# Value windows loaded as 64 and 32 rows, with the rows between zeroed on chip for the first batch, and a new order table

## The chip, the cores and the metric

The kernel runs on one core of one Trainium2 chip. The metric is device time in microseconds (us) of one execution; lower is better. Before the change three runs gave 452.86 us as the median (451.57 to 452.99).

TensorE (PE in the profile) multiplies matrices, VectorE (DVE), ScalarE (ACT) and GpSimd (POOL) work element by element, and SyncE (SP) issues all transfers. Each engine runs its own instructions in the order in which the program lists them, and waits for other engines and for transfers at semaphores.

## The reference

Attention over 8 heads feeds a gated two-layer network. Everything is float32 except the three weight matrices, which arrive as 64-bit numbers.

```python
# attention: q, k, v are (4, 8, 768, 64); block = 32, window = 16
k_sum = k.reshape(B, H, nb, block, D).max(axis=3)
v_sum = v.reshape(B, H, nb, block, D).mean(axis=3)
scores_l = scale * np.matmul(q, k.transpose(0, 1, 3, 2))
mask_l = np.abs(pos[:, None] - pos[None, :]) < window
scores_s = scale * np.einsum('bhsd,bhnd->bhsn', q, k_sum) + np.log(block)
scores_all = np.concatenate([np.where(mask_l, scores_l, -1e9), scores_s], axis=-1)
a = softmax(scores_all)                      # over 768 + 24 columns
x = a @ np.concatenate([v, v_sum], axis=2)   # heads side by side: (4, 768, 512)
# network: d_model 512, d_ff 1024
x_prev = x shifted by one token, zeros first
xk, xr = mu_k * x + (1 - mu_k) * x_prev, mu_r * x + (1 - mu_r) * x_prev
out = sigmoid(xr @ w_r) * (np.maximum(xk @ w_k, 0) ** 2 @ w_v)
```

Each query sees its neighbours within 15 positions and, besides, 24 block keys (the maximum of 32 keys each), whose values are the 24 block means.

## The kernel before

**Attention.** Two heads share the 128 partitions, so a batch has 4 pairs. The 768 tokens are 12 windows of 64 queries. A window uses 120 keys: 64 of its own stretch, the 24 block keys, and the 32 that follow. The array of values lies in memory in the same pattern, 128 rows a window: rows 0 to 63, then 24 rows of zeros (64 to 87), then 32 rows (88 to 119), and 8 rows more of zeros. `load_set` (L391) brings, for one pair of heads, the keys (`kt`, L398) and the values of two half sequences (`vx`, L403, one transfer of all 128 rows and 384 KB each). VectorE takes maxima of the keys (L423 to L431) and writes the 24 block keys into the gaps (L435, on VectorE or GpSimd). The 24 rows of block means go into rows 64 to 87 of the values: in the first batch TensorE sums the windows (L447), ScalarE and TensorE move the sums (L454 to L457) and GpSimd or VectorE spreads them over the windows (L461); in the later batches VectorE sums a second, transposed copy of the values (L379, L381), TensorE turns it (L384), and a transfer from `vm` to `vx` spreads the means (L468).

`unit` (L473) is the attention of one pair of heads and one half sequence, 32 of them in all: 24 small score products (L487), mask and maximum on VectorE (L497), exponential on ScalarE (L501), a division by the sum (L512, L518 or L523), three transposes on TensorE a head (L535), copies out (L541, L543), 24 small products with the values (L550), and a copy out (L564, L565).

**Network.** Three products stand for each product of full precision: weights and activations are split into a high and a low part. The weights are made from 64-bit words on chip in 20 pieces (L318 to L361) during the first batch, by VectorE, ScalarE and GpSimd. For each batch and half sequence `gate` (L629, products at L637 to L639) and `experts` (L654, products at L666 and L691, the last ones at L717) do the dense work.

**Order.** A planner records about 1930 operations. The table `ORDER` (L65) lists them in the order in which they are to be issued, with a letter where an operation goes to an engine other than its usual one (D, A, P). `schedule` (L200) walks through the table with assumed lengths (`LENGTH`, L39), mode changes (`SWITCH`, L54) and latencies, and assigns buffers; the engines keep that order. Its start times serve one more purpose: where the plan sees TensorE idle ahead of the first large products, L763 puts products of a zeroed tile with itself (`av<-still`, L764, called products on zeros here), one per 230 ns of planned idle time. They compute nothing that is used.

The lines that set this, in short:

```python
            if b or not SPLIT:
                op("SP", "load", lambda hf=hf: nc.sync.dma_start(
                    out=vw[hf].t[:, 0:S].rearrange("p (w d) -> p w d", d=P), in_=v[b, p, hf]), ...)
                continue
            op("POOL", "vzero", zeros(nc.gpsimd), writes=[(vw[hf], "b")], other=("DVE", "vzero_d", zeros(nc.vector)))
            for x, lo, hi in (("a", 0, QW), ("c", KB, NK)):
                op("SP", "load", lambda hf=hf, lo=lo, hi=hi: nc.sync.dma_start(...))
```

Of the kernel before, what the change touches and what calls it, by code (L numbers as in the profile page):

```python
# [29 lines left out]
HW = NW // 2  # L30
NSL = HW // 2
HT = S // 2
# [7 lines left out]
    score=776, transpose=245, vtrans=82, vpool=800, vsel=75, values=848, mixe=1400, gate=2780, gate_p=2085, e1=2085,  # L40
    e2a=1390, e2b=695, e2=695, e2h=350,
# [12 lines left out]
SWITCH = dict(MS=100, SM=112, MV=108, VM=112, TM=85, ST=55, VT=55, TS=175, TV=175)  # L54
LATENCY = dict(M=201, S=265, V=236, T=228, DVE=115, ACT=133, POOL=180, SP=0)
# [3 lines left out]
WARM = 230  # L59
# [7 lines left out]
209 215 217 254 79 11P 13 7D 60 279 72 14 61 8 218 219 43 221 6 15P 42 44 54D 220 45 230 55 16 53 222 304 34 241 231  # L67
223 81 80 237 239 233 33P 224 26 235 35 92 56 232 238 236 242 3 234 36 27 57P 240 28 225D 62 29 243 30 244 58 63 37 38
64 31D 245 9D 226 65 246 46 247 2 47 228 48 255 248 83 82 49 419 51 249 328 400 256 250 99 727 257 266 84 262 260 85P
264 258 267 261 265 50 280 259 263 420 251 74 283 291 401 281 287 285 73P 268 269 289 284 66 282 75 253A 305 67 270D  # L70
68 271D 76 292 290 272 403 69 609 286 312 273D 70 288 106 316 314 402 274 71 421 293 423 86 308 294 275 94 310 306 93
276 422 87 296 95 295D 424 88 329 89 299 412 302 277 90 332 300D 352 101 309 278A 404 405 334 425 701 1169 307 317 315
426 297 120 427 298 311 406 102 96 97 428 413 108 340 313 407 336 330 98 408 338 100P 318 335 337 333 77 319 320 109
113 301 103 78 353 303A 322 104 409 122D 321D 107D 668 105 431 341 339 331 148 110 414 323 123 410 342 115 354 358 411
343 356 121P 111 429 324 415 432 344 430 433 325 112 116 345 326 124 114 434 346 127 376 134 125P 435 362 364 360 150D
126 417 347 151 149 117 327A 436 162 667 152 118 136D 129D 119 418 153 437 447 440 416 135 438A 137 154 130 348 349
448 141 377 138 613 164D 439 139 350 365 441 128D 165 669 176 725 618 445 140 131 446 454 163P 380 388 382 351 143 449
442 363 355 450A 155 166 132P 641 378 384 386 443A 361 359 452 444 133 451 144 455 357 379 366 367 142D 178D 387 381
389 502 369 498 453 461 462 368D 167D 179 169 385 383 168 145 459 372 373 463 177 460 612 157 370 371 390D 468 503 158
391 180 676 601 146 464A 181 614 392D 394 456 393 374 499 615 182 619 465 395 670 156P 469 396 457A 500 475 91 643 197  # L80
626 630 624 397 671 171D 159 458 620 375A 504 160 506 147 398 501 628 476 466 611 399A 161 622 510 629 470 631 507 467
511 473 508 505 512 509 513 623 170 474 172 621 471A 514 173 183 199D 477 174 198 200 625 627 175 729 190 480 472 201
602 185 481 515 632D 186 672 184 516 605 603 187 528 188 478A 192D 673 189 193 479 520 633 487 517 191 194 529 202 518
610 599 524 195 525 634 196 521 604 644 526 519 527 636 530D 783 482 522 532 531 533 637 534 653 523 488 535 483 203
600 484 485A 562 1173 486 649 651 647 606 495 496 492 607 489 493 490 536 555 654 650 608 728 648 652 655 730 645 646
656 635 657D 658 1113 617 734 616 638 537 677 639D 660 686 538 640 678 682 688 684 679 689 539A 687 659P 663 642 680
541 664D 683 540 542 543 681 685 548 556D 544 545 690 557 661 691 549D 692P 702 662 699 693P 786 665 1053 675 1045 841
1172 842 731P 694 666 757 674 1487 546 707 703 713 785 695 704 550 759 1062 791 705 547 551 709 708 553 843D 706 1174
711 863D 710 554 712 714 696 715 735 697 552 716 1057 558 718D 717 698 792 744 1056 726 732 497 491 719 700A 742 560
787 563 743 745 559 788 740 789P 738 736 569 741 720 815 845P 737 746 739 747 846 1058 1059 864 748 721 749 750P 760  # L90
722D 494 733 751D 723 763 817 1497 784 765 570 766 752 561 761 1049 771 865 767 768 567 769 844 770 753D 764 867P 762
568 847D 772 866 773D 754 564 724 793 755 774 775D 565A 571 756 776P 798 804 794 777 800 576 802 801 790 848 1229 1046
795 758A 778 796 797 849P 779 574 566 1500 577 578 799 1501 871D 805 803 583 575 579A 868 780D 806 572 807 580 850 872
1050 781 818 584D 808 829 1111 821 573 585 810 825 823 819 1171 1112 581 811 1175 809 782A 827 1043 822 1047 582 1502
586A 1087 1236 812 828 1063 826 820 813D 814 869D 1064 824 851 1070 1072 1073 830 588 1085 1066 816A 1074 587 852 1075
589 853P 831 1067 832 834D 854 593 596 855 856 1048 1114 875P 1068 837 590 833 591 1065 876 838 1069 1071 877D 861 594
1044 878 835 873D 874 597 1088 836 598 839 1051 859 1052 1118 592 595 1095 1091 870 884 857 1115 1076 1092 942 1177
1077 943 1099 1488 1227 1097 1089 1119 860 879 1054 1120 1503 858 946D 1078D 1098 1231 880D 947 1096 1100 948 1060 881
1079D 1116 1117 1145 885D 886 882A 944D 1235 887 1090 883 950D 840A 1093 945 968D 888 969 951 891 892 862 898 919 1080
1259 920D 893 1081 952 953 972D 1121 1130 949 1094 1082 889 1132 890 1126 1128 896 1124 894A 895 1101 973 1122 1230  # L100
899 1129 1083 1133 954D 905 897 900 901 1125 1127 1170 902 955 903 1123 956D 1102 1103D 921 1131 1134D 957 906 907 904
964D 965 1146 908A 1135 1055 909 1104D 1084 1105 1556 1491 912 1157 1178 1153 1158 913 1613 1106D 1154 1061 1203 910
1136D 958 911 1107 917 959 914 960 1151 1108 915 1617 916 1155 1137 1149 1147 922A 1086A 918 1138 961 962 1150 1148
1156 924 974D 975 923 1152 963 1109 976 1179 1139 966 1616 1140 926 1618 977 978 1232 1186 1180 1182 1110A 967 1188
925 1159 1189 1160 1619 927 928 970D 929A 1141 1161D 931 1190 979 1184 1285D 1286 1287D 1185 1191 932 1204 1187 1162D
1492 1142 1555 971 1261 1489 1176 1163 930 933 936 980 1181 1164 1183 1192D 1559 1193 1194P 1143 1493 1165 1195 981
1144A 982 1213 1205 1206 939 992 1166 1311P 983A 1703 934 1558 937 938 1499 1560 1561P 985 1209 984 1210 1288 993 1215
1312 1307 940 999 986D 987 1313D 1214 1308 988A 994 989 990 1233 1000 1211 1207 1001 1289 1314 1290 991 1196 1167 1208
# [762 lines left out]
```

## Time and profile before

| | |
|---|---|
| median of three runs | 452.86 us |
| the profiled execution, its own time | 453.34 us |
| its span, first to last instruction | 451.5 us |
| TensorE busy | 443.9 us (98% of the span) |
| VectorE, ScalarE, GpSimd busy | 295.9, 284.2, 45.9 us |
| mean granted TensorE clock | 0.999 |
| products on zeros, in the trace | 122 records, 18.2 us |
| transfers | 51.95 MB; 43.28 MB read from memory |

Times in the views are microseconds from the span's first instruction unless marked ns. In a row of the timeline the first number is the start, the second how long it lasted, then come engine, line, operation, what is written `<-` what is read, shapes, and the count of instructions merged; a bracket gives idle time before it and what ended that. A float32 product of the listing is two records in the trace. Records of TensorE overlap, so the distance from start to start tells what one costs. In the views by windows each engine has its busy time and its number of instructions, then the granted clock, the share of the transfer engines in use, and GB/s.

### The profile page before, as it was taken

To read this page: it belongs to the slowest core of one execution; us is meant where nothing else is said; L and a number is where in the kernel's file an instruction comes from. 1 tells how busy PE (TensorE), PEld (TensorE's weight loads), DVE (VectorE), ACT (ScalarE), POOL (GpSimd) and SP (SyncE) were. 2 spreads that over 40 slices of the span, in tenths; PEclk is the share of its full clock that TensorE was granted. 3 is DMA by queue.
4 is the path that set the end of the run, shared out by engine and by line. 5 is a ranking of instruction groups with operands and counts; after the bars stand their busy time and mean duration, and the time that the engine had idled before them with its cause. 6 is when DMAs were issued, how large, how long until landed. Compare 5 with 4: busy or idle time off the path is not lost.

```text
span 451.5 us, 9681 instructions
## 1 busy us (share of the span) xinstructions
PE 443.9 (98%) x3608; PEld 381.6 (85%) x3608; DVE 295.9 (66%) x944; ACT 284.2 (63%) x843; POOL 45.9 (10%) x96
## 2 busy tenths in 40 slices
PE   9999999999999999999999999999999999999996
PEld 8867888789888789888988879888889888989985
DVE  2999999997887877828677676358364533445131
ACT  2889999987775849569574586466675434232211
POOL 0443222000230100000200001011002000000000
PEclk9999999999999999999999999999999999999999
DMA  8976684551557543240723112105100000003002
GB/s 311 403 262 221 208 326 131 179 208 33 145 169 217 220 132 91 85 147 1 221 73 120 53 56 84 43 19 177 48 2 0 2 0 1 0 1 116 1 0 93
DMA packets 26878, 51.95 MB, mean 115 GB/s; under 512 B 2512, under 2 KB 14416, under 8 KB 26832
## 3 DMA queue, kind: packets, MB, share of 16 engines
q1 hardware_dynamic: 26832, 51.35, 33.8%
q8 instruction: 28, 0.46, 0.4%
q14 instruction: 18, 0.15, 0.1%
HBM read 43.28 MB, written 6.29 MB: 110 GB/s over the span
## 4 chain that ended last, share of the span: by engine, by line
PE 76%; DVE 9%; ACT 8%; DMA 3%; issue 2%; SPq 1%; DVEq 0%; POOL 0%; POOLq 0%
PE mm L666 25%; PE mm L691 23%; PE av L550 4%; PE pt L535 4%; PE mm L637 4%; PE mm L639 4%; PE mm L638 4%; PE sc L487 4%; PE mm L717 3%; DMA kt<-in_k 2%; ACT y L501 2%; PE av L764 2%; DMA vx<-vm 1%; DVE y L497 1%; DVE we L336 1%
## 5 line engine op out<-in xcount | busy, mean ns | idle before, releaser
L666 PE MATMUL mm<-xs,wk_h 128*128 128x384 f32 x512 | 101.4, 340 | 0.0
L501 ACT ACTIVATE y<-y,mn 128x120 f32<-128x120 f32 x192 | 74.1, 388 | 30.5 <-DVE mn L497 30.1
L666 PEld LDWEIGHTS mm<-xs,wk_h 128*128 128x128 f32 x512 | 89.6, 188 | 3.7 <-ACT r L672 0.8
L691 PE MATMUL mm<-wv_h,kh 128*128 128x512 f32 x168 | 67.5, 402 | 0.0
L691 PE MATMUL mm<-wv_l,kh 128*128 128x512 f32 x168 | 66.3, 395 | 0.0
L497 DVE CUSTOM_DVE_ANT_0 y<-sc,fixed_sb 128x120 f32<-128x120 f32 x192 | 46.5, 276 | 25.5 <-PE pt L535 13.3
L666 PE MATMUL mm<-xs,wk_l 128*128 128x384 f32 x256 | 55.2, 337 | 0.0
L676 ACT ACTIVATE r<-r 128x384 f32<-128x384 f32 x64 | 32.9, 521 | 27.7 <-DVE r L674 27.2
L691 PE MATMUL mm<-wv_h,kl 128*128 128x512 f32 x168 | 49.1, 401 | 0.5 <-DVE kl L681 0.5
L681 DVE TENSOR_TENSOR kl<-r,kh 128x384 fp32r<-128x384 f32 x64 | 35.3, 556 | 19.1 <-ACT kh L680 11.1
L666 PEld LDWEIGHTS mm<-xs,wk_l 128*128 128x128 f32 x256 | 45.5, 188 | 0.0
L672 ACT ACTIVATE r<-mm 128x384 f32<-128x384 f32 x39 | 19.1, 489 | 38.8 <-PE mm L666 31.0
L590 DVE SCALAR_TENSOR_TENSOR xa<-vx,fixed_sb,xa 128x384 f32<-128x384 f32 x60 | 37.0, 622 | 9.1 <-ACT xa L583 7.4
L637 PE MATMUL mm<-wr_h,xs 128*128 128x512 f32 x96 | 39.0, 407 | 0.0
L639 PE MATMUL mm<-wr_h,xs 128*128 128x512 f32 x96 | 38.0, 396 | 0.0
L638 PE MATMUL mm<-wr_l,xs 128*128 128x512 f32 x96 | 37.9, 395 | 0.0
L596 DVE TENSOR_TENSOR xs<-xa,xs 128x384 fp32r<-128x384 f32 x60 | 33.0, 558 | 6.9 <-ACT xs L593 5.6
L691 PEld LDWEIGHTS mm<-wv_h,kh 128*128 128x128 f32 x168 | 31.6, 188 | 6.5 <-ACT kh L680 0.4
L691 PEld LDWEIGHTS mm<-wv_l,kh 128*128 128x128 f32 x168 | 31.6, 188 | 6.0
L501 ACT ACTIVATION_READ_ACCUMULATOR y<-y,mn 128x1 f32 x192 | 36.5, 190 | 0.0
L691 PEld LDWEIGHTS mm<-wv_h,kl 128*128 128x128 f32 x168 | 30.7, 188 | 6.8 <-DVE kl L681 0.9
L535 PE MATMUL pt<-fixed_sb,y 128*120 128x128 f32 x192 | 33.1, 281 | 0.1
(88 smaller groups left out, 699.2 us busy)
## 6 DMA issues: line engine op xcount, KB each, us to landing
vx<-in_v SPq DMA_DIRECT2D x32, 384.0 KB, 4.1
kt<-in_k SPq DMA_DIRECT2D x15, 544.0 KB, 4.9
qt<-in_q SPq DMA_DIRECT2D x32, 192.0 KB, 3.8
out<-z SPq DMA_DIRECT2D x23, 256.0 KB, 4.2
st<-in_vT SPq DMA_DIRECT2D x12, 384.0 KB, 4.5
st<-in_w_k SPq DMA_DIRECT2D x8, 512.0 KB
st<-in_w_v SPq DMA_DIRECT2D x8, 512.0 KB
st<-in_w_r SPq DMA_DIRECT2D x4, 512.0 KB, 8.0
```

Of the source, the lines that this page charges most:

```text
L497: op("DVE", "mask", lambda h=h, i=i, var=var: nc.vector.tensor_tensor_reduce(out=y[h].t[:, i, :], in0=sc[h].t[:, i, 0:NK], in1=mask_sb[:, ...
L501: op("ACT", "exp", lambda h=h, i=i: nc.scalar.activation(y[h].t[:, i, :], y[h].t[:, i, :], AF.Exp, bias=mn[h].t[:, i:i + 1], scale=-1.0, a ...
L535: nc.tensor.transpose(out=pt.t[0:NK, i * P:(i + 1) * P], in_=y[h].t[:, i, :], identity=ident_sb)
L590: op("DVE", "mixd", lambda xt=xt, xa=xa, p=p: nc.vector.scalar_tensor_tensor(out=xa.t, in0=xt.t[:, 1 + lo:1 + lo + HT], scalar=mu_sb[:, wh ...
L596: op("DVE", "sub", lambda xa=xa, xh=xh, xl=xl: nc.vector.tensor_tensor(out=xl.t, in0=xa.t, in1=xh.t.bitcast(F32), op=ALU.subtract), reads= ...
L637: nc.tensor.matmul(ps[t].t, xh.t[:, ts], wr_h[:, p, :], start=(p == 0), stop=False)
L638: nc.tensor.matmul(ps[t].t, xh.t[:, ts], wr_l[:, p, :], start=False, stop=False)
L639: nc.tensor.matmul(ps[t].t, xl.t[:, ts], wr_h[:, p, :], start=False, stop=(p == NPAIR - 1))
L666: nc.tensor.matmul(ps.t[:, 0:HT], w[:, j, p, :], x[p][s].t, start=(n == 0), stop=(n == 11))
L676: op("ACT", "square", lambda: nc.scalar.activation(r.t, r.t, AF.Square), reads=[(r, 0)], writes=[(r, 0)])
L681: op("DVE", "sub", lambda: nc.vector.tensor_tensor(out=kl.t, in0=r.t, in1=kh.t.bitcast(F32), op=ALU.subtract), reads=[(r, 0), (kh, 0)], wr ...
L691: nc.tensor.matmul(acc[t].t, a.t[:, t * P:(t + 1) * P], w[:, j, :], start=start, stop=stop)
```

## The change

The values come in two transfers a half sequence in all four batches: rows 0 to 63 (192 KB) and rows 88 to 119 (96 KB). Rows 64 to 87 and the last 8 rows are no longer read. In the first batch rows 64 to 87 are set to zero on chip, since TensorE sums whole windows there; in the later batches nothing is written there before the block means arrive, so that the transfer of means no longer follows a load of the same rows. That takes 32 transfers more and 96 KB less for each of the 32 half sequences, and 8 zeroings, 6 on GpSimd and 2 on VectorE.

The planner's numbers change: dense products a little longer, shorter latencies after scores and values and a longer one after transposes, no cost for the change from values to dense products, later landings of transfers, and more time for issuing the transfer of means. A product on zeros now counts 430 ns up to 6 us and 230 ns after that, and the first one is planned from 1.0 us. Their number falls from 61 to 49.

```diff
-SWITCH = dict(MS=100, SM=112, MV=108, VM=112, TM=85, ST=55, VT=55, TS=175, TV=175)
-LATENCY = dict(M=201, S=265, V=236, T=228, DVE=115, ACT=133, POOL=180, SP=0)
+SWITCH = dict(MS=100, SM=112, MV=108, TM=55, TS=175, TV=175)
+LATENCY = dict(M=201, S=130, V=120, T=300, DVE=115, ACT=133, POOL=180, SP=0)
...
-WARM = 230
+WARM, WARM_COLD, COLD = 230, 430, 6000
...
-SPLIT = 0
+SPLIT = 2
+LATE = 400
...
-252 227 17 18 204 0 10 39 52 21 229 32 22 23 24 25 20 19 205 59 41 40 206 212 1 210 208 216 213 207 5D 211 4D 12D 214
+71 68D 47 22 293 92 18 17 220 0 10 43 60 27 26 25 28 29P 19 245 36 24 20 21 23 221 67 45 49 48 46 1 222 223 9 224 228
...
-                now[e] = start + DMA_ISSUE
+                now[e] = start + DMA_ISSUE + o.more[0]
                 dma = max(dma, start + DMA_START) + DMA_EACH + o.size / DMA_BYTES_PER_NS
-                o.finish = dma + DMA_END
+                o.finish = dma + DMA_END + o.more[1]
...
-            if b or not SPLIT:
+            if SPLIT == 0 or SPLIT == 1 and b == 0:
...
-            op("POOL", "vzero", zeros(nc.gpsimd), writes=[(vw[hf], "b")], other=("DVE", "vzero_d", zeros(nc.vector)))
+            if b == 0:
+                op("POOL", "vzero", zeros(nc.gpsimd), writes=[(vw[hf], "b")], other=("DVE", "vzero_d", zeros(nc.vector)))
...
-    end, early = 600, True
+    end, early = 1000, True
     for o in order:
         if o.eng == "PE" and early:
-            for _ in range(int((o.start - end) // WARM)):
+            for _ in range(int(max(0, o.start - max(end, COLD)) // WARM + max(0, min(o.start, COLD) - end) // WARM_COLD)):
                 nc.tensor.matmul(spare, still, still, start=True, stop=True)
```

The table `ORDER` is new throughout, and the same code stands 3 or 4 lines further down (L487 is L491, L764 is L768). Three places show what it does.

TensorE, from its first instruction to the scores of the second pair of heads, before (`sc` is the scores, `kt` and `qt` keys and queries):

```order
L764 MATMUL av0_146<-still_160 128x128 x21
L487 MATMUL sc0_143<-kt0_61,qt0_65 64x120 x2
L487 MATMUL sc1_144<-kt0_61,qt0_65 64x120 x2
...
L764 MATMUL av0_146<-still_160 128x128 x25
L487 MATMUL sc0_143<-kt1_62,qt1_66 64x120 x2
```

and now:

```order
L768 MATMUL av0_146<-still_160 128x128 x11
L491 MATMUL sc0_143<-kt0_61,qt0_65 64x120 x2
L491 MATMUL sc1_144<-kt0_61,qt0_65 64x120 x2
...
L768 MATMUL av0_146<-still_160 128x128 x23
L491 MATMUL sc1_144<-kt1_62,qt1_66 64x120 x2
```

Ahead of the first scores 21 products on zeros became 11, and ahead of the second 25 became 23; from there to the scores of the third pair there are 15 in both.

GpSimd, from its first tile to the first weights, before (`wc`, `we` and `wr_h` belong to the weights):

```order
L758 MEMSET still_160 128x128
L558 MEMSET vx0_68 128x1
L558 MEMSET vx1_69 128x1
L328 ISA
L328 TENSOR_SCALAR wc0_141<-st0_136 128x512
L358 TENSOR_SCALAR wr_h_157<-wc0_141 128x512
```

and now:

```order
L762 MEMSET still_160 128x128
L412 MEMSET vx0_68 24x768
L412 MEMSET vx2_70 24x768
L412 MEMSET vx3_71 24x768
L562 MEMSET vx4_72 128x1
L412 MEMSET vx5_73 24x768
L439 COPY kt0_61<-ks0_80 128x12x24
L412 MEMSET vx6_74 24x768
L335 ISA
L335 TENSOR_SCALAR we0_139<-st0_136 128x512
L361 TENSOR_SCALAR wr_h_157<-wc0_141 128x512
```

Five zeroings come ahead of the first weights on GpSimd (one more stands at the start of VectorE's row, ahead of the first maxima of keys), and the block keys of the first pair, which VectorE wrote before (L435), are written here behind four of them. The scaling of the first weights (`wc0`) went from GpSimd to ScalarE.

SyncE, the values of the first pairs, before:

```order
L318 DMA st2_138<-in_w_r 128x1024
L403 DMA vx2_70<-in_v 128x768
L403 DMA vx3_71<-in_v 128x768
L398 DMA kt2_63<-in_k 128x1088
L403 DMA vx4_72<-in_v 128x768
L403 DMA vx5_73<-in_v 128x768
L476 DMA qt2_67<-in_q 128x384
L398 DMA kt3_64<-in_k 128x1088
L403 DMA vx6_74<-in_v 128x768
```

and now:

```order
L321 DMA st2_138<-in_w_r 128x1024
L417 DMA vx3_71<-in_v 32x768
L417 DMA vx6_74<-in_v 64x768
L417 DMA vx6_74<-in_v 32x768
L417 DMA vx3_71<-in_v 64x768
L401 DMA kt2_63<-in_k 128x1088
L417 DMA vx7_75<-in_v 64x768
L417 DMA vx2_70<-in_v 32x768
L417 DMA vx2_70<-in_v 64x768
L417 DMA vx7_75<-in_v 32x768
L401 DMA kt3_64<-in_k 128x1088
L480 DMA qt2_67<-in_q 128x384
```

The eight transfers ahead of these rows are the same, but for the two pieces of the first keys, which changed places. Each load of values became two, and the keys of the third and fourth pair stand behind the same number of half sequences as before.

Over the whole program the same attention and network operations remain, but some change engines: divisions by the sum on GpSimd fall from 10 to 4 and on VectorE from 29 to 25 and rise on ScalarE from 25 to 35; loads of ScalarE's function tables fall from 22 to 18. On TensorE the dense products are cut up differently: they are followed at once by scores or values 30 times instead of 17, and values are followed at once by dense products 18 times instead of 4.

More of the change, by code (lines that the diff above doesn't have):

```diff
@@ L39 @@
 LENGTH = dict(
-    score=776, transpose=245, vtrans=82, vpool=800, vsel=75, values=848, mixe=1400, gate=2780, gate_p=2085, e1=2085,
-    e2a=1390, e2b=695, e2=695, e2h=350,
+    score=776, transpose=245, vtrans=30, vpool=800, vsel=320, values=848, mixe=1400, gate=2797, gate_p=2095, e1=2095,
+    e2a=1398, e2b=700, e2=700, e2h=350,
     kred=862, kred2=460, kmax=75, kcopy=225, vred=865, mask=203, eps_d=72, rc=100, norm3=448, evac=470, pts_d=468,
@@ L70 @@
[L70 to L89, printed above, removed]
@@ L105 @@
[L105 to L108, printed above, removed]
-1237 995A 1197 1168A 1216 1212 1198 1217 1246 1238 1506 1622 941 1494 1239 997 935 1242 1243 998 1244 1199 1248 1249
@@ L141 @@
+1917 1936 1884D 1918 1921 1922 1919 1923 1924 1925 1927 1926 1928D 1885 1929 1932 1933 1948 1930A 1937A 1938 1939 1931
+1949 1940 1941 1942 1946 1943 1950 1944 1945 1886 1947 1953 1887 1951A 1952 1955 1954 1956 1960 1957 1958 1959 1961
+1962 1965 1888 1889 1963 1966 1890 1967 1964 1515 1968 1891 1971 1969 1972 1970 1973
 """
@@ L151, with __init__ @@
 class Op:
-    def __init__(self, n, ways, bufs, size):
-        self.n, self.ways, self.bufs, self.size = n, ways, bufs, size
+    def __init__(self, n, ways, bufs, size, more):
+        self.n, self.ways, self.bufs, self.size, self.more = n, ways, bufs, size, more
         self.deps, self.start, self.finish, self.eng = set(), None, None, None
@@ L170, in buf, with op @@
         return Buf(pool, n)
-    def op(self, eng, kind, emit, reads=(), writes=(), size=0, other=()):
+    def op(self, eng, kind, emit, reads=(), writes=(), size=0, other=(), more=(0, 0)):
         bufs = []
@@ L181, in op @@
             ways = {e: w for e, w in ways.items() if w[0] not in BAN}
-        o = Op(len(self.ops), ways, bufs, size)
+        o = Op(len(self.ops), ways, bufs, size, more)
         o.tag, o.name = self.tag, kind
@@ L379, in block_means @@
             op("SP", "load", lambda p=p, tokens=tokens: nc.sync.dma_start(out=tokens(), in_=vT[b - 1, p]),
-               writes=[(vt, 0)], size=P * S * 4)
+               writes=[(vt, 0)], size=P * S * 4, more=(0, LATE))
             op("DVE", "vred", lambda p=p, tokens=tokens: nc.vector.tensor_reduce(
@@ L414, in load_set @@
                     out=vw[hf].t[lo:hi, 0:S].rearrange("p (w d) -> p w d", d=P), in_=v[b, p, hf, lo:hi]),
-                   writes=[(vw[hf], x)], size=(hi - lo) * HW * 512)
+                   writes=[(vw[hf], x)], size=(hi - lo) * HW * 512, more=(0, LATE if b else 0))
         def blocks():
@@ L469, in load_set @@
                     out=windows(x)[QW:KB], in_=means.t[NS * p:NS * p + NS].unsqueeze(1).broadcast_to([NS, HW, P])),
-                   reads=[(means, 0)], writes=[(x, "b")], size=NS * HW * 512)
+                   reads=[(means, 0)], writes=[(x, "b")], size=4 * NS * HW * 512, more=(480, 0))
         return e
@@ L476, in unit @@
         op("SP", "load", lambda: nc.sync.dma_start(out=qt.t, in_=q[b, p, :, hf * HT:(hf + 1) * HT]),
-           writes=[(qt, 0)], size=P * HT * 4)
+           writes=[(qt, 0)], size=P * HT * 4, more=(0, LATE if b else 0))
         sc, y, mn, pts = [[buf(x) for _ in range(2)] for x in ("sc", "y", "mn", "pts")]
```

126 lines of the change are left out of this document (75 added, 51 removed).

## Prediction

> **What bounds the kernel now.** I read the busy time by windows first, then the timeline of the start, then the waits of TensorE.
>
> The windows of the whole span (TensorE, its weight loads, VectorE, ScalarE, GpSimd):
>
> ```profile
> 0.00:25.00 25.00, 23.47 (x255) 21.35 (x255) 16.92 (x60) 13.85 (x50) 5.39 (x13) 1.00 0.95 360
> 25.00:65.00 40.00, 39.90 (x455) 31.45 (x454) 38.10 (x135) 39.17 (x124) 14.42 (x21) 1.00 0.72 245
> 65.00:200.00 135.00, 132.92 (x1124) 113.17 (x1125) 109.13 (x352) 102.12 (x314) 13.30 (x31) 1.00 0.46 152
> 200.00:448.00 248.00, 247.64 (x1779) 215.60 (x1777) 131.29 (x398) 129.06 (x356) 12.76 (x31) 1.00 0.15 49
> ```
>
> From 25 us on TensorE is idle for 0.1 + 2.1 + 0.4 us in all, so the time is TensorE's work plus its start and its end. Between 25 and 65 us ScalarE (39.17 of 40 us) and VectorE (38.10) are full as well: what comes later there makes TensorE wait. Behind 200 us both are about half idle. The start is different, since its busy time is mostly products on zeros. By lines they are
>
> ```profile
> L764 PE MATMUL av<-still 128*128 128x128 f32 x122 | 18.2, 313 | 1.5 <-POOL still L758 1.0 <-DVE vx L564 0.5
> ```
>
> The timeline of the start:
>
> ```profile
> 0.99 7.85 PE L764 MATMUL av<-still 128*128 128x128 f32 x42 [0.99 <-POOL still L758]
> ...
> 5.17 0.31 DVE L435 COPY kt<-ks 128x288 f32<-128x288 f32 x1
> ...
> 8.78 0.85 PE L487 MATMUL sc<-kt,qt 64*64 64x120 f32 x24
> ...
> 9.55 5.85 PE L764 MATMUL av<-still 128*128 128x128 f32 x50
> 9.68 0.28 DVE L497 CUSTOM_DVE_ANT_0 y<-sc,fixed_sb 128x120 f32<-128x120 f32 x1 [4.20 <-PE sc L487]
> ...
> 10.21 0.40 ACT L501 ACTIVATE y<-y,mn 128x120 f32<-128x120 f32 x1 [8.19 <-DVE mn L497]
> ...
> 15.33 0.85 PE L487 MATMUL sc<-kt,qt 64*64 64x120 f32 x24
> ...
> 23.55 0.30 DVE L435 COPY kt<-ks 128x288 f32<-128x288 f32 x1
> ...
> 24.38 0.49 PE L764 MATMUL av<-still 128*128 128x128 f32 x2 [0.54 <-DVE vx L564]
> ...
> 25.13 0.85 PE L487 MATMUL sc<-kt,qt 64*64 64x120 f32 x24
> ```
>
> The first keys are complete at 5.48 us, and their scores start at 8.78, when the first 21 products on zeros are through. VectorE had stood for 4.20 us, ScalarE for 8.19. The queries of that score are the other thing that it needs:
>
> ```profile
> L476 SPq DMA_DIRECT2D qt<-in_q x1: 432/432/432, 1.6 to 1.6; - x1
> ...
> DMA to landing us min/median/max: 4.5/4.5/4.5
> ```
>
> They land at 1.64 + 4.5, say 6.2 us. So the products on zeros hold up the first scores by 2.6 us, and everything in the chain behind them.
>
> **The change part by part.** *Ten products fewer ahead of the first scores.* The windows of L764 alone give their pace, 218 ns a record up to 7.1 us (28 in 6.11) and 106 ns after it (16 in 1.70), though the granted clock reads 1.00 in both:
>
> ```profile
> 0.00:7.10 7.10, 6.11 (x28) 6.11 (x29) 1.00 0.75 252
> 7.10:8.80 1.70, 1.70 (x16) 1.55 (x14) 1.00 1.03 417
> ```
>
> Eleven products are 22 records, 4.8 us, and end at 5.8. The scores then start at 6.2 to 6.3, when the queries have landed; the block keys, which GpSimd now writes behind four zeroings, are near that too (below). But the scores run in the slow phase until 7.1: 0.85 us there do what 0.41 would, so the first mask comes 0.9 + 0.4 us behind the start, at 7.6 instead of 9.68. I count -2.1 us. Without the slow phase it would be -2.5; with a start at 6.8 it would be -1.8.
>
> The Trainium skill (TensorE: Matmul & The Clock Gate, Part 1) says that the array runs at half rate until about 3.4 us of sustained activity and again after an idle window of that length, and that the window runs freely. By that figure, as an estimate, the scores at 6.2 us would be at full rate and the term -2.5 us. The trace's 7.1 us, 6.1 after the first product, is longer than the figure, and I go by the trace.
>
> *The zeroings.* The nearest row is the spread over the same 24x768 elements:
>
> ```profile
> 20.62 0.82 POOL L461 COPY vx<-vm 24x768 f32<-24x768 f32 x1 [0.68 <-ACT vm L457]
> ```
>
> Four of them from 0.9 us end at 4.2 us, ahead of the maxima of keys at 5.2, and the copy behind them is hidden by the wait for the queries: cost nothing. If one took 1.2 us, they would end at 5.7 and the scores would start 0.3 us later. The zeroing on VectorE lies in a time when it waits for keys. The other ones on GpSimd fall into its 19.6 idle us of the first 25; the second on VectorE is counted with its row.
>
> *From the first mask to the third pair's scores at 25.13.* VectorE is the chain here. By the order it does the same work up to its 24th mask: one zeroing and one copy out of `pt` more, one sign, one copy of block keys and one copy of `av` less. So the shift of 2.1 us stays. TensorE has 23 products (46 records at 117 ns, 5.4 us) behind the first scores and then 15, as before, so they don't block it. At the end TensorE loses more than VectorE: the third keys are ready at 23.85, but the scores wait 1.28 us, since a product on zeros ahead of them waits for VectorE to copy `av`. ScalarE does that copy now, sooner in its row. I take half, -0.6 (0 to -1.2).
>
> *ScalarE up to the first gate.* The scaling of a piece of weights, by lines from 9 to 65 us:
>
> ```profile
> L325 ACT ACTIVATE wc<-st 128x512 f32<-128x512 f32 x5 | 3.4, 689 | 0.0
> ```
>
> By the order ScalarE does three of these more, 2.1 us; the other shifts cancel. It starts 2.1 us earlier and has slack until 25 us (13.85 busy), not behind it. I take +0.3 (0 to +2.1).
>
> *Transfers.* A window of the start, whose last two columns are the transfer engines' share and GB/s:
>
> ```profile
> 10.00:15.00 5.00, 5.00 (x47) 5.00 (x46) 4.96 (x23) 4.28 (x19) 1.38 (x2) 1.00 1.02 408
> ```
>
> Then the issues (size, us to landing), and SyncE's wait at the transfer of means (total, times, longest):
>
> ```profile
> vx<-in_v SPq DMA_DIRECT2D x32, 384.0 KB, 4.1
> qt<-in_q SPq DMA_DIRECT2D x32, 192.0 KB, 3.8
> ```
>
> ```profile
> SPq L468 <- DMA vx<-in_v: 27.5, 9, 4.8
> ```
>
> The transfer engines are full in the start at 408 GB/s. Eight half sequences of 96 KB less are 768 KB, 1.9 us less to move, so data doesn't fall behind a chain that is 2 us earlier. Later the means no longer wait for a load: 27.5 us of SyncE's waits go. What was queued behind them (queries, keys) goes out earlier; 32 issues come in, at some 0.43 us each as that of the queries above. Nothing of that is on TensorE's path but the wait of 0.4 us below.
>
> The Trainium skill (DMA: Bandwidth & Descriptors, Anatomy of one DMA) speaks against small pieces: about 2 us fixed for each, of which 96 KB would need only 0.2 more. By that, as an estimate, a lone 96 KB reaches a tenth of the rate. Here eight are in flight and 408 GB/s is reached with pieces of 192 KB among them; the trace's own 3.8 us for 192 KB against 4.1 for 384 also says that a landing hardly depends on size.
>
> *Mode changes on TensorE.* Three stretches give the prices, from start to start:
>
> ```profile
> 48.32 0.49 PE L535 MATMUL pt<-fixed_sb,y 128*120 128x128 f32 x3
> 48.57 0.48 PE L637 MATMUL mm<-wr_h,xs 128*128 128x512 f32 x1
> 48.88 0.40 PE L638 MATMUL mm<-wr_l,xs 128*128 128x512 f32 x1
> ...
> 58.33 0.49 PE L535 MATMUL pt<-fixed_sb,y 128*120 128x128 f32 x3
> 58.74 0.85 PE L487 MATMUL sc<-kt,qt 64*64 64x120 f32 x24
> ...
> 60.37 0.50 PE L691 MATMUL mm<-wv_h,kh 128*128 128x512 f32 x1
> 60.71 0.39 PE L691 MATMUL mm<-wv_l,kh 128*128 128x512 f32 x1
> 60.94 0.40 PE L691 MATMUL mm<-wv_h,kh 128*128 128x512 f32 x1
> ...
> 95.75 0.40 PE L639 MATMUL mm<-wr_h,xs 128*128 128x512 f32 x1
> 96.08 0.85 PE L487 MATMUL sc<-kt,qt 64*64 64x120 f32 x24
> 96.85 0.54 PE L535 MATMUL pt<-fixed_sb,y 128*120 128x128 f32 x3
> 97.15 1.11 PE L666 MATMUL mm<-xs,wk_h 128*128 128x384 f32 x5
> ```
>
> A dense product takes 0.23 us among its like, 0.33 ahead of scores or values, 0.34 behind values, 0.31 behind transposes. A group of transposes takes 0.25 between dense products, 0.30 behind scores, 0.41 ahead of them. Counted through the order: dense ahead of scores or values 17 to 30 times (13 x 0.10 = +1.3), dense behind values 4 to 18 (+1.5), dense behind transposes 42 to 55 (+1.0), transposes ahead of scores or values 15 to 2 (13 x 0.16 = -2.1), transposes behind them 31 to 19 (-0.6). Together +1.1 us. It is the one certain loss.
>
> *Waits in the middle.*
>
> ```profile
> PE av L550 <- DVE pts L543: 0.6, 1, 0.6
> PE mm L691 <- DVE kl L681: 0.5, 1, 0.5
> PE av L550 <- DMA vx<-vm: 0.4, 1, 0.4
> ```
>
> The window 65 to 200 us has 2.1 us idle. The last wait ends with the freed means; the others depend on the new order, which I can't price. I take -1.0, from -2.0 to +1.
>
> The sum: -2.1 - 0.6 + 0.3 + 1.1 - 1.0 = -2.3 us. The profiled execution took 453.34 us, 1.84 more than its span and 0.5 more than the median; 453.34 would become 451.0 and the median of 452.86 becomes **450.6 us**.
>
> **The rivals.** About 0.3% (1.36 us) is what a measurement of this kernel can tell from no change.
>
> *Small pieces take the place of the products (no change).* By the program's semaphores SyncE sends a transfer when the one eight places earlier has landed. Rows 10 to 33 of its new order move 5,194 KB in 24 pieces, 216 KB on average: eight of those in 4.1 us are 432 GB/s, just above the 408 of the row. If a landing takes 5 us, the rate is 354, and these rows take 15.0 instead of 13.0 us: 2.0 us that eat the gain, 452.6 us. For it speaks that 3.8 and 4.1 us are so close; against it, that VectorE, and no landing, ended the waits in the start.
>
> *All of the products' time is saved.* The 98 records left take 4.8 + 76 x 0.117 = 13.7 us instead of 18.2. If every engine follows, the start gives -4.5 instead of -2.4: 448.5 us. For it speaks the 8.19 us that ScalarE stood, against it the full VectorE.
>
> *New waits in the three later batches (slower).* Each of 24 units there now waits for two pieces of values and the means, sent at different places of SyncE's row (of one half sequence of the second batch, 64 rows stand at row 41 and 32 rows at row 61), and scores, values and dense products alternate with less between. Without the -1.0 for the middle the gain is 1.3 us; units that wait 0.4 us like the one above use it up at the fourth, and from the seventh on the kernel is slower by more than 0.3%. If half of them wait, it is 452.86 - 1.3 + 12 x 0.4 = 456.4 us. Against it speaks the transfer engines' share, 0.46 and less after 65 us.
>
> **How the numbers follow.** Forecast 0.52, small pieces 0.18, all saved 0.17, new waits 0.13. Faster: 0.48 + 0.17 = 0.65. Same: 0.04 + 0.16 + 0.03 = 0.23. Slower: 0.02 + 0.10 = 0.12. The range goes from 448.0, all saved with a little of the middle, to 453.3, small pieces with a little more wait in the middle; it leaves out the new waits and a part of the others.
>
> **What would show it.** The first scores of the profile after start at 6.2 to 6.8 us and the first mask at 7.6; the third pair's scores at about 22.5 instead of 25.13; products on zeros 98 records, 13 to 14 us; idle time of TensorE between 65 and 200 us about 1 us; the dense products behind values at 0.34. The forecast is wrong if TensorE shows idle time of over 2 us before 25 us, or waits for `vx` in the later batches that add up to more than 3 us.

## The result and the profile after

The changed kernel takes 454.63 us (median of 20 runs, 451.93 to 458.01), the kernel before beside it 452.11 us (451.14 to 454.21). The ratio is 1.0051, with a 95% interval from 1.0031 to 1.0070: slower by 0.5%, about 2.3 us, where the forecast was 2.3 us faster. The profiled execution took 455.25 us, with a span of 453.4 us.

The windows of the changed kernel, with the columns of the prediction's (TensorE, its weight loads, VectorE, ScalarE, GpSimd, clock, share of the transfer engines, GB/s):

```profile
0.00:25.00 25.00, 21.96 (x259) 19.39 (x260) 18.29 (x63) 16.06 (x54) 9.82 (x21) 1.00 0.95 272
25.00:65.00 40.00, 35.54 (x411) 27.66 (x410) 34.78 (x118) 35.65 (x114) 11.16 (x17) 1.00 0.84 243
65.00:200.00 135.00, 134.12 (x1137) 113.94 (x1136) 113.00 (x372) 106.89 (x331) 12.13 (x23) 1.00 0.52 153
200.00:448.00 248.00, 248.00 (x1774) 215.21 (x1773) 130.75 (x404) 126.95 (x359) 8.66 (x22) 1.00 0.15 42
```

From 65 us on TensorE is idle less than before (0.9 us instead of 2.1 + 0.4). The loss lies ahead of that: 4.46 us idle from 25 to 65, where it was 0.1. Read the last two columns of the first row: the transfer engines are as full as before (0.95), but move 272 GB/s instead of 360. A share says how long packets were under way, not how much they brought.

What TensorE waits for (total, times, longest):

```profile
PE mm L451 <- DMA vx<-in_v: 4.3, 4, 1.9
PE sc L491 <- DMA qt<-in_q: 1.9, 2, 1.3
```

L451 are the block sums of the first batch, which need all rows of the values. In the timeline the first scores start at 5.82 us, before the 6.2 to 6.8 of the forecast, and the first mask at 6.72 instead of 7.6. By the third pair's scores a part of that is lost (23.55, where about 22.5 was forecast and 25.13 stood before), and the last block sums are late:

```profile
0.98 4.91 PE L768 MATMUL av<-still 128*128 128x128 f32 x22 [0.98 <-POOL still L762]
5.82 0.85 PE L491 MATMUL sc<-kt,qt 64*64 64x120 f32 x24
6.59 5.40 PE L768 MATMUL av<-still 128*128 128x128 f32 x46
...
23.55 0.85 PE L491 MATMUL sc<-kt,qt 64*64 64x120 f32 x24
...
36.62 0.96 PE L451 MATMUL mm<-vx,fixed_sb 120*32 120x128 f32 x24 [1.94 <-DMA vx<-in_v]
```

The chain of waits up to there (start, length, what) is one of transfers, each of which was only sent when the one eight places earlier had landed:

```profile
4.92 9.09 DMA st<-in_w_r
14.01 0.02 issue
14.03 7.28 DMA vx<-in_v
21.31 0.02 issue
21.33 9.01 DMA vx<-in_v
30.33 0.02 issue
30.35 6.22 DMA vx<-in_v
```

They land after 6 to 9 us, not 4 or 5. The GB/s of the stretch from 5 to 37 us, in 40 slices of 0.8 us, show since when; first the kernel before, then the changed one:

```profile
GB/s 371 422 384 412 416 405 429 402 396 424 428 388 385 406 421 411 401 389 403 401 394 396 396 388 366 288 78 108 206 262 365 405 101 65 245 385 365 338 363 77
```

```profile
GB/s 311 400 394 411 409 405 417 387 232 212 191 233 202 223 228 203 208 256 229 234 344 395 362 292 198 215 181 194 196 209 246 266 236 261 244 246 301 246 372 394
```

Some 400 GB/s until 11.4 us, and mostly about half of that from the first pieces of values on, whose first packet starts at 10.7 us. From 21.0 to 23.4 us, when only 15 of their packets start, the rate is back at 344 to 395. By 25 us 272 x 25 us = 6.8 MB have come, before 9.0; the pieces spare 0.8 MB of that, so 1.4 MB are missing, 3.4 us at 408 GB/s.

An account of TensorE up to the first dense product of the first gate, in us, from the records of each profiled execution (products on zeros, by count and us, and other work from start to start; idle: gaps over 0.15 us; the first product stands at 0.98 or 0.99). The names of the experiments stand below.

```
                        products on zeros  other work  idle  first dense product
before                    122   17.65        17.57     0.54        36.75
changed                    98   14.13        18.12     6.53        39.76
fewer products alone      102   14.79        17.57     0.79        34.13
... and pieces            102   14.41        18.19     3.84        37.43
changed, 1st batch whole  112   15.27        16.95     0.61        33.82
```

So the change saved 3.5 us of products, added 0.55 us of other work and 6.0 us of waiting, +3.0 together. Behind that product TensorE works 408.76 us before and 408.79 after, and is idle 2.13 and 0.88 us by the windows: -1.2. The sum, +1.8, is the difference of the spans (451.5 and 453.4).

### The profile page after: what moved, and what is told of

It is laid out like the page before. It is cut to its first block, busy times and chain, and to the rows that moved or that the text cites. A ratio compares the mean times of both kernels' runs of the same rounds, so it can differ in the third digit from the quotient of the medians.

```text
span 453.4 us, 9689 instructions
## 1 busy us (share of the span) xinstructions
PE 441.0 (97%) x3584; PEld 377.3 (83%) x3584; DVE 297.6 (66%) x955; ACT 286.1 (63%) x857; POOL 41.8 (9%) x83
## 4 chain that ended last, share of the span: by engine, by line
PE 88%; DMA 8%; SPq 2%; issue 0%; ACT 0%; DVE 0%; DVEq 0%
PE mm L670 29%; PE mm L695 25%; PE av L554 5%; PE mm L641 5%; DMA vx<-in_v 5%; PE mm L643 5%; PE mm L642 5%; PE pt L539 4%; PE sc L491 4%; PE mm L721 4%; DMA st<-in_w_r 2%; DMA qt<-in_q 1%; SPq L417 1%; PE mm L618 1%; SPq L480 0%
## 5 line engine op out<-in xcount | busy, mean ns | idle before, releaser
L501 DVE CUSTOM_DVE_ANT_0 y<-sc,fixed_sb 128x120 f32<-128x120 f32 x192 | 47.6, 276 | 17.7 <-PE sc L491 9.0
L676 ACT ACTIVATE r<-mm 128x384 f32<-128x384 f32 x45 | 22.1, 491 | 53.7 <-PE mm L670 48.0
L683 DVE CAST kh<-r 128x384 fp32r<-128x384 f32 x32 | 11.7, 365 | 41.9 <-ACT r L680 35.1
```

The lines of the kernel that those rows point to most:

```text
L501: op("DVE", "mask", lambda h=h, i=i, var=var: nc.vector.tensor_tensor_reduce(out=y[h].t[:, i, :], in0=sc[h].t[:, i, 0:NK], in1=mask_sb[:, ...
```

## The experiments

Times are medians, with the ratio to the kernel before, run on the same chip, and its 95% interval.

### The parts one by one

**Fewer products alone** (kernel before):

```diff
-            for _ in range(int((o.start - end) // WARM)):
+            n = int((o.start - end) // WARM)
+            for _ in range(n - 10 if n == 21 else n):
```

> The kernel before with its order and its whole value transfers, but 11 instead of 21 products on zeros ahead of the first scores. Every theory says that the first scores start at about 6.2 us. If the prediction's first term is right by itself, the third pair's scores start at 22.5 to 23.0 instead of 25.13 and the time is 450.0 to 450.5 us against 452.1. If the start is bound by the transfers, which run full at 400 GB/s there, the third pair stays at 25 and the time at 451.8 to 452.3.

449.42 us, 0.9939 (0.9918 to 0.9959). Its timeline, TensorE and VectorE:

```profile
22.52 0.85 PE L487 MATMUL sc<-kt,qt 64*64 64x120 f32 x24
...
7.10 0.28 DVE L497 CUSTOM_DVE_ANT_0 y<-sc,fixed_sb 128x120 f32<-128x120 f32 x1 [1.67 <-DMA fixed_sb<-in_fixed]
```

The third pair's scores come 2.6 us earlier, and so does the first dense product (34.13 instead of 36.75). The prediction's first term, -2.1, is there by itself, with 0.5 us to spare.

**Pieces alone** (kernel before; the rows between are zeroed once at the start, in five tiles by GpSimd and in five by VectorE):

```diff
-                op("SP", "load", lambda hf=hf: nc.sync.dma_start(
-                    out=vw[hf].t[:, 0:S].rearrange("p (w d) -> p w d", d=P), in_=v[b, p, hf]),
...
+                def pieces(hf=hf):
+                    for lo, hi in ((0, QW), (KB, NK)):
+                        nc.sync.dma_start(
+                            out=vw[hf].t[lo:hi, 0:S].rearrange("p (w d) -> p w d", d=P), in_=v[b, p, hf, lo:hi])
+                op("SP", "load", pieces,
...
+    for n, t in enumerate(pools["vx"]):
+        (nc.vector if n % 2 else nc.gpsimd).memset(t[QW:KB, 0:S], 0.0)
```

> The kernel before with its order and its 21 products, but each value transfer sent as 64 and 32 rows one behind the other, the rows between zeroed once at the start. Theory of narrow transfers (pieces on 64 or 32 partitions keep the transfer engines as busy while moving half as much): packets of 3,072 bytes take 200 to 240 ns on average before 30 us instead of 124, TensorE idles 3 us or more before 65 us, 454 to 456 us. Rival of the count (eight in flight, each transfer with a fixed cost): packets stay at 125 to 140 ns, the engines' share falls below 0.9, and the time is also 453 to 456. Rival of the order (the new order alone brings the waits): 451.5 to 452.5 us.

455.24 us, 1.0065 (1.0039 to 1.0091). The pieces alone cost 3 us, in the order before and with 25% fewer bytes of values. Packets of 3,072 bytes took 190 ns before 30 us, a little less than I had said. But the place is not the one expected: the first dense product comes at 36.39, no later than before, with 0.85 us idle ahead of it. (Its 122 products on zeros took 16.94 us instead of 17.65, since their pace changed at 5.6 us in this execution and at 7.1 in that of the kernel before.) The profile's loss stands later:

```profile
PE mm L669 <- ACT r L675: 2.1, 1, 2.1
PE pt L538 <- ACT pts L544: 1.2, 1, 1.2
```

Both lie behind 170 us, and the chain of waits leads from each back to keys of a later batch:

```profile
165.59 4.65 DMA kt<-in_k
...
213.45 6.06 DMA kt<-in_k
```

Why those keys hold up this kernel, and not the one with the same pieces in the later batches alone (below), is open.

**Fewer products and pieces**, both changes in the order before:

> The order before with 11 products and with the values in 64 and 32 rows: the changed kernel without its new order. If the effects add up: 452.1 - 2.7 + 3.2 = 452.6 us, and the new order costs the changed kernel 2 us more. If the pieces take all of the products' gain: 454.5 to 455.5, and the new order costs nothing.

451.63 us, 0.9977 (0.9957 to 0.9997), a microsecond below the first case: the pieces take 2.2 of the 2.7 us. Not all of that need be theirs. VectorE's five zeroings stand ahead of the first maxima of keys and keep it from 0.96 to 4.89 us, so that the first pair's block keys come late, and TensorE waits for them:

```profile
6.60 0.84 PE L490 MATMUL sc<-kt,qt 64*64 64x120 f32 x24 [1.14 <-DVE kt L438]
```

Without the pieces and zeroings these scores start at 5.83. How much of the 0.8 us reaches the end is not shown; with 21 products the same delay hides behind them. The same products and pieces cost 454.6 us in the new order; more on that below.

**The new order with whole transfers** (in the first batch):

```diff
...
-            for x, lo, hi in (("a", 0, QW), ("c", KB, NK)):
+            if b == 0:
+                pieces = ("a", 0, P), ("c", 0, 0)
+            else:
+                pieces = ("a", 0, QW), ("c", KB, NK)
+            for x, lo, hi in pieces:
...
```

(with nothing sent for `c`, and no zeroing, in the first batch)

> The kernel after with its order and its 11 products; the first batch's values as whole 128 rows where their 64 rows stood, without its 32 rows and its zeroings, the three later batches still in 64 and 32 rows. Theory of narrow transfers: the 6.5 us that TensorE stands between 10 and 65 us in the profile after fall to under 1.5, the middle stays at about 0.9 idle, 449 to 450.5 us. Theory that the new order is at fault too: 4 us or more of waits stay somewhere before 200 us, 452 to 454 us.

449.92 us, 0.9950 (0.9934 to 0.9967). The windows:

```profile
0.00:25.00 25.00, 23.41 (x293) 20.10 (x293) 18.46 (x72) 17.98 (x64) 8.48 (x19) 1.00 0.95 358
25.00:65.00 40.00, 40.00 (x423) 32.54 (x420) 38.46 (x129) 39.32 (x126) 9.97 (x16) 1.00 0.73 238
65.00:200.00 135.00, 132.60 (x1169) 112.50 (x1168) 108.18 (x354) 101.44 (x312) 10.66 (x22) 1.00 0.51 145
```

358 GB/s instead of 272, no idle time from 25 to 65 us, and 4.7 us won back by eight transfers that carry a third more bytes. (The zeroings are gone with them, and the planner puts 112 records of products on zeros instead of 98.) The middle did not stay at 0.9 us idle, as I had said: it is 2.4, of which TensorE waits 1.3 for queries and 1.1 for a copy by ScalarE. An earlier form used whole transfers in all four batches:

> The kernel after with its order and its 11 products, but 128 rows in one transfer where its 64 rows stood, none for its 32 rows, and no zeroing. Narrow transfers or count: TensorE's waits for values between 10 and 65 us fall from some 6 us to under 1.5, packets of 3,072 bytes take about 125 ns, 449.5 to 450.8 us. Order: the waits stay at 4 us or more and the time at 453.5 to 455.

452.35 us, 1.0016 (0.9997 to 1.0036). The waits of the start went as expected, but 4.7 us of others came between 65 and 200 us. There the new order sends the freed means of some half sequences ahead of their values, and the whole transfer writes zeros over them, so part of the later batches' means is lost. As a test of the later batches it says nothing; the next one does.

**Pieces in the later batches alone** (order before, fewer products):

```diff
...
+                    for lo, hi in ((0, QW), (KB, NK)) if b else ((0, P),):
...
```

> The order before with 11 products; values of the first batch whole, those of the three later batches in 64 and 32 rows. If narrow transfers only hurt where the transfer engines are full: 449.2 to 450.2 us, as without pieces (449.4). If the new waits of the prediction's third rival are real: idle time of TensorE behind 65 us of 3 us or more, and 451 to 453 us.

449.56 us, 0.9943 (0.9923 to 0.9962), with 0.78 us idle from 65 to 200:

```profile
65.00:200.00 135.00, 134.22 (x1134) 114.49 (x1133) 108.76 (x353) 103.11 (x311) 13.21 (x31) 1.00 0.48 142
```

Where the transfer engines are half empty the same pieces cost nothing. They also gain nothing that can be told from the 449.42 us without them.

### What makes a piece slow

Transfers of values with nothing beside them:

```diff
+STAGES = (
+    ("whole", 12, lambda i: (0, P, 0, HW)),
+    ("low64", 12, lambda i: (0, QW, 0, HW)),
+    ("rows32", 12, lambda i: (KB, NK, 0, HW)),
+    ("halves", 12, lambda i: (QW * (i % 2), QW * (i % 2) + QW, 0, HW)),
+    ("narrow", 12, lambda i: (0, P, 0, HW // 2)),
+    ("mixed", 12, lambda i: ((0, QW, 0, HW), (KB, NK, 0, HW))[i % 2]),
+    ("rows120", 12, lambda i: (0, NK, 0, HW)),
...
```

> Only transfers of values, in eight stages of twelve with a wait between stages (the output is left without a meaning): whole 128 rows; rows 0 to 63; rows 88 to 119; rows 0 to 63 and 64 to 127 in turn; 128 rows of half width (1,536 bytes a row); 64 and 32 rows in turn; 120 rows; rows 64 to 127. Narrow transfers: whole 390 to 410 GB/s, rows 0 to 63 some 200, 32 rows 100 to 130, the two halves in turn 380 to 410, half width 350 to 400, 64 and 32 in turn below 200. Count: rows 0 to 63, the halves in turn and half width, all of 192 KB, run alike, at 250 to 390, and 32 rows at half of that, with packets of 3,072 bytes at 121 to 130 ns everywhere.

One window from within each of the first seven stages, in that order; the last two columns are the transfer engines' share and GB/s:

```profile
4.00:15.00 11.00, 0.00 (x0) 0.00 (x0) 1.00 0.96 367
19.00:29.00 10.00, 0.00 (x0) 0.00 (x0) 1.00 0.93 187
32.00:36.50 4.50, 0.00 (x0) 0.00 (x0) 1.00 0.69 197
40.50:49.00 8.50, 0.00 (x0) 0.00 (x0) 1.00 0.95 220
52.00:59.00 7.00, 0.00 (x0) 0.00 (x0) 1.00 0.88 289
63.00:69.00 6.00, 0.00 (x0) 0.00 (x0) 1.00 0.83 238
74.00:90.00 16.00, 0.00 (x0) 0.00 (x0) 1.00 0.97 228
```

Whole transfers run at 367 GB/s (I had said 390 to 410), 64 rows at 187 with the engines as full; and the time of one 3,072-byte packet is 127 ns against 240 on average. That is the loss in the kernel, where such packets took 124 ns before and 229 after (between 5 and 30 us). (The eighth stage, rows 64 to 127, overlaps with the stores behind it; its packets took 240 ns too.) Two halves in turn do not make up for one another (220, where I had said 380 to 410). Half width is slower than whole transfers as well, 289 instead of the 350 to 400 that I had said, but much faster than 64 rows with as many bytes. The 32 rows were held by the issues, 12 in 5.45 us, as SyncE's queue shows:

```profile
29.63 5.45 SPq L271 DMA_DIRECT2D vx<-in_v  x12
```

and half their packets took 121 ns, so my 100 to 130 GB/s for them was too low, and 64 and 32 in turn reach 238, where I had said below 200.

The Trainium skill (SBUF — State Buffer, Door 1: The DMA port swizzle) says that a transfer's rate depends on how many of 16 ports its partitions reach, that partitions 0 to 63 reach eight of them, and gives 196 GB/s for these and 328 for all 128, measured at 1 MiB. The trace agrees in kind, with 187 and 367 for 192 and 384 KB. But 120 rows run at 228, little better than 64, though by the page's table rows 0 to 119 touch every port. So the count of ports alone does not explain the 120 rows; of the shapes with 64 rows or more, only those with all 128 were fast here.

In the kernel, with as many transfers and bytes in the one as in the other, two transfers per half sequence of 128 rows and three windows:

```diff
...
+                    for lo, hi in ((0, HW // 2), (HW // 2, HW)):
+                        nc.sync.dma_start(
+                            out=vw[hf].t[:, lo * P:hi * P].rearrange("p (w d) -> p w d", d=P), in_=v[b, p, hf, :, lo:hi])
...
```

> The kernel before, each value transfer cut into two of 128 rows and three windows (1,536 bytes a row). Narrow transfers: packets of 1,536 bytes take 65 to 80 ns and the time is 452 to 453 us, no more than 1 us above the kernel before. Count of transfers: as slow as the 64 and 32 rows sent alone, 454 to 456.

and of 64 rows and all windows, `((0, QW), (QW, P))` in the diff of the pieces alone:

> The kernel before, each value transfer cut into rows 0 to 63 and rows 64 to 127, so as many transfers and bytes as with the two wide ones. Narrow transfers, and that a transfer behind it on the other half does not make up for it: packets of 3,072 bytes take 180 to 230 ns before 30 us, and the time is 456 to 459 us, since the start moves 8 times 192 KB more than with 64 and 32 rows. If the two halves made up for one another: 452 to 453.

and one transfer of 120 rows, `vw[hf].t[0:NK, 0:S]` from `v[b, p, hf, 0:NK]`:

> The kernel before, each value transfer with rows 0 to 119 in place of 0 to 127 (the last 8 are read by nothing). If it were the part of the partitions that a transfer covers, 120 of 128 cost 7% at most, which the 6% fewer bytes pay: 452 us. If what counts is that each transfer engine has rows of its own, which only the full 128 gave in the transfers alone (228 against 400 GB/s): packets of 3,072 bytes at 180 to 220 ns before 30 us, and 456 to 465 us, as with the two halves.

They take 452.27 us, 1.0003 (0.9986 to 1.0020); 464.72 us, 1.0263 (1.0228 to 1.0299); 458.93 us, 1.0142 (1.0114 to 1.0169). The first 25 us of the three, wide first:

```profile
0.00:25.00 25.00, 23.48 (x281) 21.07 (x282) 17.24 (x61) 14.65 (x52) 5.90 (x14) 1.00 0.95 337
```

```profile
0.00:25.00 25.00, 23.66 (x279) 21.34 (x279) 16.49 (x60) 14.35 (x52) 5.38 (x13) 1.00 0.94 277
```

```profile
0.00:25.00 25.00, 21.11 (x250) 19.30 (x251) 16.11 (x58) 13.30 (x49) 4.96 (x13) 1.00 0.94 265
```

Twice as many transfers cost no time that can be measured, if each has all 128 rows, though the rate of the start falls from 360 to 337 GB/s. As many with 64 rows cost 12.6 us, more than I had said. And leaving out eight rows that nothing reads costs 6.3 us. The count of transfers is out as the cause of the loss; the rows of one decide. Packets of 3,072 bytes took 194 ns in the halves and 204 with 120 rows. The Trainium skill (SBUF — State Buffer, "Can I just issue two DMAs to hit both halves?") answers no, and the two halves agree: 220 GB/s in turn against 187 for one half alone.

### Why the new order pays more for them

With whole transfers in the first batch both orders take about the same (449.4 and 449.9), with pieces 451.6 and 454.6. By SyncE's rows, the new order sends 704 KB more than the old one up to the last values of the first batch (a 512 KB piece of key weights and one more transfer of queries, 192 KB). First I sent two pieces of weights later in the new order:

```diff
+    for weights, behind in ((28, 32), (20, 25)):
+        places.remove(loads[weights])
+        places.insert(places.index(loads[behind]) + 1, loads[weights])
```

> The changed kernel with two pieces of weights of 512 KB sent later: the fourth piece of the receptance weights behind the values of the third pair, the first piece of the key weights behind those of the fourth pair. If the new order costs its 3 us against the old one (454.6 to 451.6 with pieces in both) because these 512 KB stand ahead of values that TensorE waits for, the first dense product of the first gate comes at 37 to 38 instead of 39.76 and the time is 451.8 to 452.8. If the weights are as urgent, since ScalarE, VectorE and GpSimd then stand for them, the first dense product stays at 39.5 to 41 and the time at 454 to 456.

455.83 us, 1.0080 (1.0057 to 1.0104); the first dense product at 39.84. The idle time ahead of it fell by 2.7 us, but the planner put 22 records of products on zeros there, and a new chain stands in its place:

```profile
21.43 8.12 DMA st<-in_w_r
29.62 0.09 issue
29.73 0.10 POOL we L335
29.83 0.49 issue
30.32 0.43 POOL kt L439
30.80 0.84 PE sc L491 x24
```

The receptance weights now land at 29.6; their sign stands on GpSimd ahead of the copy of block keys, and the fourth pair's first scores, at 27.50 in the changed kernel, wait for that copy until 30.80. So I had moved one piece too many. Then the key weights alone, with the products held at their number, in the new order (behind the values, `loads[28]` behind `loads[32]`), and the reverse in the old order with pieces (ahead of the fourth pair's values):

> The changed kernel with its products as they are; only the first piece of the key weights (512 KB) is sent behind the fourth pair's values, the receptance weights stay where they were. If the 704 KB more (key weights and one transfer of queries) that the new order sends ahead of the last values are its cost: the last wait for values (1.94 us at 36.6) goes, the first dense product comes at 37.3 to 38.3 instead of 39.76, 452.5 to 453.3 us. If the order's cost lies elsewhere: 39.3 to 40 and 454 to 455.5 us.

> The order before with 11 products and pieces, as in the earlier run of 451.63 us, but the same 512 KB of key weights sent ahead of the fourth pair's values instead of behind them. If that is what the new order costs: a wait for values of 1.5 us or more ahead of the fourth pair's block sums, the first dense product at 39 to 39.8 instead of 37.43, 453.0 to 454.3 us. If not: 451 to 452.2 us.

453.32 us, 1.0030 (1.0007 to 1.0053), and 453.48 us, 1.0028 (1.0011 to 1.0046). TensorE's waits for values, with the key weights behind them in the new order, then in the old order as it was and with the key weights ahead:

```profile
PE mm L451 <- DMA vx<-in_v: 0.5, 2, 0.3
```

```profile
PE mm L450 <- DMA vx<-in_v: 2.3, 3, 1.1
```

```profile
PE mm L450 <- DMA vx<-in_v: 3.7, 3, 1.7
```

In the old order the place of these 512 KB is worth 1.9 us (451.63 to 453.48, intervals apart), in the new one 1.3 us by the medians, where the intervals of the ratios overlap. In the new order's profile the first dense product came at 35.4, earlier than I had said; the median gained less than that, and TensorE is idle 1.4 us longer behind that product than in the changed kernel (2.3 against 0.9). In the old order's it came at 38.26, where I had said 39 to 39.8. So the place of the key weights is shown as one cause in the old order, and likely in the new one; the rest, one or two us, stays open. It may be more, since the runs in the old order with pieces also carry the late block keys of their zeroings.

## Why the prediction was wrong

**The step that failed** is the paragraph on transfers: "data doesn't fall behind a chain that is 2 us earlier". It rested on 408 GB/s being "reached with pieces of 192 KB among them", and on landings that hardly depend on size. Both rows were right, but those 192 KB were queries: 128 rows of 1,536 bytes. The 192 KB of values are 64 rows of 3,072. I compared sizes where the shape decided, and no row of the profile before had a large transfer on fewer than 128 rows. Its nearest one, the means on 24 rows, was in the groups and I didn't use it. So the transfers stood at nothing in the sum. They cost 4.7 us: 454.63 us against 449.92 with the first batch's values whole, with 229 ns for a 3,072-byte packet where it had been 124. The fixed 2 us that the prediction takes from the Trainium skill (DMA: Bandwidth & Descriptors, Anatomy of one DMA) are given there for transfers issued by GpSimd. In the transfers alone SyncE's pieces of 96 KB landed 2.3 us after their issue in the median, close to that price.

**The rival that came closest** is small pieces in the place of the products. Its mechanism, the eighth place earlier that has to land, is the chain of the profile after; its landing of 5 us was 6 to 9, so that it took not the products' gain alone but 2.3 us more. I had it as no change at a chance of 0.18. (The 24 pieces that it adds up make 5,184 KB, not 5,194, which changes nothing.) The slower rival, new waits for values in three later batches, did not happen: TensorE's waits for values are all in the first batch, and pieces in the later batches alone cost nothing. (The order before with pieces in all batches did lose 3 us to keys behind 160 us, another mechanism, and not in the changed kernel.)

**The start** (-2.1 and -0.6) was right where the transfers allow it, and a little too small. With the fewer products alone, in the old order, the third pair's scores come 2.6 us earlier; with the new order and the first batch whole they start at 21.66, another 0.9 earlier. In the changed kernel they start at 23.55; two waits for values are 1.2 us of the difference. The steps inside are less right than the sum. The first scores start at 5.82, not at 6.2, since the queries have landed by then. They take 0.77 us to the next record, as at 8.78 before, so the surcharge of 0.4 us for the slow phase did not come: the pace of TensorE had changed by then, not at 7.1. That was the luck of this execution. With pieces in the later batches alone the same scores started at 5.98, still in the slow phase, and took 1.27 us. And the first mask waits for the transfer of the masks, a wait that the prediction doesn't have: until 6.64 in the changed kernel, until 7.10 with the fewer products alone. **The zeroings** cost nothing, as forecast: the scores at 5.82 wait for nothing.

**Waits in the middle** went from 2.1 to 0.9 us between 65 and 200, forecast -1.0, but that is luck. The wait for the freed means (0.4) did go. The other waits are not the order's doing alone: with the fewer products alone, in the old order, the middle is idle for 0.7 us, and with the new order and the first batch whole for 2.4.

**Mode changes** (+1.1, "the one certain loss") came to nothing, though each price held. Behind the first dense product, a dense product ahead of scores or values took 0.33 us in the median, behind values 0.34, behind transposes 0.31, in both kernels. By kind of work, from start to start, the dense products took 341.4 us before and 344.2 after, +2.8 where the prediction had +3.8; the transposes took 18.3 and 15.4, -2.9 where it had -2.7. So the term that it called certain was too large by the dense part. **ScalarE's** +0.3 did not show either: with the first batch whole TensorE does not stand between 25 and 65 us. The sign of error that the prediction named, over 2 us of idle time before 25 us, is met: 25 - 21.96 = 3.04, where it was 1.53 before.

**The best version** of those run is the smallest change: ten products fewer in the kernel before, 449.42 us, 2.7 us under it and 5.2 under the changed one. Pieces in the later batches besides (449.56) can't be told from it.

## What to carry to other kernels

Fewer bytes are not less time: before a transfer is cut by rows, look at how many partitions each piece covers, and compare it with transfers of the same shape, not of the same size. A full share with fewer GB/s is the mark of it (0.96 with 367 alone, 0.93 with 187); read the two columns together. A waste that fills idle time hides what it covers, so take it away alone first: here the gain was whole by itself, and the rest of the change gave it back.

## What the runs showed of the hardware

- Slow transfers slow their neighbours. Between 5 and 30 us the 4,352-byte packets of the keys, on 128 rows in both kernels, took 174 ns before and 257 after, and the 1,536-byte packets of the queries 68 and 93, on 128 rows too. Within the changed kernel the keys' packets took 172 ns before the pieces came, and 309 to 337 between 10.7 and 21 us. The 4,096-byte packets of the weights, most of which started when few pieces were under way, hardly changed (168 and 174).
- 120 rows of 128 moved 228 GB/s, 128 rows 367, with packets of the same size: 208 and 127 ns. Why 120 are so much slower the runs don't show; how the packets are dealt out to the engines is not in the trace.
- SyncE issued twelve pieces of 96 KB in 5.45 us, 0.45 us each. At that pace they can't pass some 216 GB/s, an estimate from these two numbers.
- The pace of the products on zeros changes from 213 to 112 ns a record at a time that differs from one execution to the next: at 3.9 us with 120 rows, at 7.1 in the kernel before, with the granted clock at 1.00 on both sides. So a difference of a microsecond in the start of two single profiles may be no more than that; in the pieces alone it was 0.7 us.
- The changed kernel spreads more than the kernel before, in 20 runs each: 451.9 to 458.0 us against 451.1 to 454.2.
